# First expert stage of a fused attention and expert kernel: weight loads six units apart, x and Y loaded later, first second-product one unit later, a fourth buffer

## The chip, the cores and the metric

The kernel runs on one core of a Trainium2 chip. The core has five engines with queues of their own, each worked off strictly in order: PE (TensorE, matrix products), DVE (VectorE), ACT (ScalarE), POOL (GpSimd) and SP (SyncE, which here only issues DMAs). The metric is device microseconds of one execution; the time given is the median over several runs.

## The reference

The kernel computes attention with a memory term and, on its output, two expert layers:

```python
x = _attn(q, k, v, M_prev, z_prev, beta)          # 2304 tokens x 512, four batches of 576
h = x @ w_in                                      # 512 -> 2048
x = (h / (1 + exp(-h))) @ w_out                   # 2048 -> 512: the first expert layer
h = x @ w2_in                                     # 512 -> 1024
sm = softmax(h); s = h * sm
out = (layer_norm(s) * g_ln) @ w2_out             # 1024 -> 512: the second expert layer
```

All of it is float32. To run products on PE at full rate, each float32 operand is split into two parts (`xh` and `xl`, `gh` and `glo`, `w[:, :, 0]` and `w[:, :, 1]`), and each product is made of three: high by high, low by high, high by low.

## The kernel before

The first expert layer is cut by the hidden dimension into 16 chunks `f` of 128 columns (`w_in` and `w_out` of a chunk lie in one tile `w`). A **unit** is one chunk for 288 tokens (half a batch): `h_unit` makes the first product (12 matmuls into `psh`), ACT applies the activation in place and casts to `gh`, and DVE subtracts to `glo`; `m1_y` makes the second product (12 matmuls into four banks `psy0` to `psy3`: 8 with `gh`, then 4 with `glo`). Over the chunks of a **part** the four banks accumulate; after the part's last chunk they are added to `Y[b]` in SBUF (four DVE instructions `y<-y,psy`; four ACT copies in the very first part; the last two parts use another form for the activation). There is one set of four banks, so the first second-product of the next half-part can start only when these four adds are done. The list `work` holds 92 units, numbered 0 to 91 below: units 0 to 11 are chunks 0 to 5 of batch 3 (the other batches' chunks 0 to 5 were done during the attention, their sums wait in DRAM as `Yd`), units 12 to 51 are chunks 6 to 10 of all batches (half-parts of five units), 52 to 75 chunks 11 to 13 (three units), 76 to 91 chunks 14 and 15 (two units).

A chunk's weights come by `load_w` in two halves: a DMA into `wraw` (pool `wr`, two buffers), an ACT instruction and three DVE instructions that unpack the raw words into `wf` (`TENSOR_SCALAR`, two `SCALAR_TENSOR_TENSOR`), an ACT cast to the high part, a POOL subtraction for the low part; chunks 20 to 23 (second layer's `w_out`) have one more DVE instruction per half, a product with `gl`. The chunks 6 to 15 and the eight of the second layer (16 to 23) go through eleven slots (`w1p`, `w0p`), each of which can be refilled when its old chunk is used up (`free`). `x` of batches 0 and 1 and `Y` of batches 2, 0 and 1 come back from DRAM in this stage. `split_x` casts 288 tokens of x on ACT (`xh`) and subtracts on POOL (`xl`).

The program writes all operations into a list with a due number `order.prio` each; a planner (`Order.plan`) places them: at each step the engine whose next operation can start first, and on it the operation that can start first by a cost table, ties by the lower due number. What results is one fixed order per engine. The lines that the change touches:

```python
        while st["w"] < len(coming) and n + 1 >= free[st["w"]]:
            next_w()
            if n % 3:
                break
```

Of the kernel before, what the change touches and what calls it, by code (L numbers as in the profile page):

```python
# [17 lines left out]
PSUM = bass.MemoryType.PSUM  # L18
DRAM = bass.MemoryType.DRAM
SBUF = bass.MemoryType.SB  # L20
# [18 lines left out]
WARM = (100000, 1, 4000)  # L39
T_S, T_T, T_O = 20, 10.5, 21  # L40
T_A, T_B, T_P, T_G, T_Y, T_C = 8, 4, 2, 1, 2.5, 1
P0 = 6
W1 = 5

# [4 lines left out]
class Sym:  # L49


    def __init__(self, buf, ap, path=()):
        self.buf, self.ap, self.path = buf, ap, path
# [80 lines left out]
class Order:  # L134
# [7 lines left out]
    def __init__(self, scratch):  # L142
        self.scratch, self.made, self.rings, self.ops, self.prio, self.least = scratch, {}, {}, [], 0, 0
        self.walls = []
        self.chain = None

    def stand_in(self, shape, dtype):
        key = (shape, str(dtype))
# [18 lines left out]
    def take(self, eng, real, method, args, kw):  # L167
        outs = [a for i, a in enumerate(args) if isinstance(a, Sym) and (i == 0 or (method == "tensor_tensor_reduce" and i == 7))]
        outs += [a for k, a in kw.items() if k in ("out", "accum_out") and isinstance(a, Sym)]
        every = [a for a in list(args) + list(kw.values()) if isinstance(a, Sym)]  # L170
        ins = [a for a in every if not any(a is o for o in outs)]
        n = len(self.ops)
        deps, raw, bufs = set(), set(), []
        for a in every:
            assert not a.buf.closed, (method, a.buf.name)
            if a.buf not in bufs:
                bufs.append(a.buf)
        for a in ins:
            c = a.cells()
            raw.update(a.buf.writer[c].tolist())  # L180
            a.buf.readers.append((n, c))
        deps.update(raw)
        for a in outs:
            c = a.cells()
            deps.update(a.buf.writer[c].tolist())
            kept = []
            for r, rc in a.buf.readers:
                if r == n:
                    kept.append((r, rc))
                    continue  # L190
                hit = np.isin(rc, c)
                if hit.any():
                    deps.add(r)
                if not hit.all():
                    kept.append((r, rc[~hit]))
            a.buf.readers = kept
            a.buf.writer[c] = n
        deps -= {-1, n}
        if self.chain is not None:

            deps.update(self.chain)
            self.chain = [n]
        reads = deps.intersection(raw)
        for b in bufs:
            b.ops.append(n)
        took, after = self.length(eng, method, args, kw, outs, ins)
        self.ops.append((eng, real, method, args, kw, deps, bufs, took, after, self.prio, self.least, reads))
# [156 lines left out]
def body(ctx, tc, qk, qk2, qt, vp, mz, beta, w1, w2i, w2o, gln, out):  # L364
# [8 lines left out]
    def f32(ap):  # L373
# [17 lines left out]
    order = Order(bacc.Bacc("TRN2", target_bir_lowering=False, num_devices=1))  # L391
    pe, dve, act, pool, sp = (order.engine(n, e) for n, e in (
        ("pe", nc.tensor), ("dve", nc.vector), ("act", nc.scalar), ("pool", nc.gpsimd), ("sp", nc.sync)))
# [5 lines left out]
    def pools(stack, **kinds):  # L399
        return [Pool(order, bufs, space, name=name, **({"side": side} if side else {}))  # L400
                for name, (bufs, space, side) in kinds.items()]
# [6 lines left out]
    xes, att = ExitStack(), ExitStack()  # L408
    kept = pools(ctx, w0p=(P0, SBUF, None), dx=(1, DRAM, None), gates=(1, SBUF, None), xsp=(1, SBUF, None))
    w0p, dx, gates, xsp = kept  # L410
# [104 lines left out]
    st = {}  # L515
    heads, raws, v_t, mem_t, s_t, unit, X, Xd, Yd = {}, {}, {}, {}, {}, {}, {}, {}, {}
# [343 lines left out]
    for b, c0, c1, z0, z1 in FILL:  # L860
        fs = range(PART[b])
        w = [(fill_split, b, c0, c1)] + [(fill_h, f) for f in fs] + [(fill_y, b, c0, c1, fs, c) for c in range(4)]
        fill += [(z0 + (z1 - z0) * n / len(w), *x) for n, x in enumerate(w)]
    ws = sorted((T_W[n] + T_W[2] * i, n, i) for i in range(P0) for n in range(2))
    calls = []
# [8 lines left out]
    for n, (z, d, u, q0, q1) in enumerate(turns):  # L874
        q = (q0, q1)
        due = dict(DUE, **T_2) if q0 else DUE if q1 == S else dict(DUE, **T_1)
        due = {k: x + (T_0 if q1 < S else 0) for k, x in due.items()}
# [11 lines left out]
        while ws and ws[0][0] < z + d:  # L889
            least = WLEAST[0] + WLEAST[1] / 2 * (2 * P0 - len(ws))  # L890
            call(z, ws[0][0] + DUE["w"], load_w, ws[0][2], w0p, p1, (ws[0][1],), least=least)
# [44 lines left out]
    mo, wes = ExitStack(), ExitStack()  # L936
    lasting = pools(ctx, yp=(1, SBUF, None), w1p=(W1, SBUF, None))
    yp, w1p = lasting
    xq, = pools(xes, xq=(1, SBUF, "right"))
    second = pools(mo, wr=(2, SBUF, None), m1=(2, SBUF, None), m3=(3, SBUF, None), m0=(1, SBUF, None), ps_h=(4, PSUM, None), ps_y=(1, PSUM, None))  # L940
    wr, m1, m3, m0, ps_h, ps_y = second

    def open_second():
# [8 lines left out]
    due = 9 * NU + 12  # L952
    order.prio = due
    Y = [yp.tile([128, NP, S], F32, tag=f"y{b}", name="y") for b in range(B)]
    for b in range(2):
        X[b] = xq.tile([128, NP, S], F32, tag=f"x{b}", name="x")
        sp.dma_start(X[b], Xd[b])

    n1 = P0 + W1
    coming = list(range(P0, NF + 8))  # L960
    before = [-1] * W1 + list(range(P0)) + coming[:len(coming) - n1]
    parts = [(b, PART[b], P0) for b in (3, 0, 1, 2) if PART[b] < P0]
    parts += [(b, f, min(f + 3, NF)) for f in (P0, n1) + tuple(range(n1 + 3, NF, 3)) if f < NF for b in (2, 3, 0, 1)]
    parts = [(b, f0, n1 if f0 == P0 else f1) for b, f0, f1 in parts]
    work = [(p, i, f) for p, (b, f0, f1) in enumerate(parts) for i in range(2) for f in range(f0, f1)]
    free = [1 + max(n for n, w in enumerate(work) if w[2] == c) if 0 <= c < NF else 0 if c < 0 else len(work)
            for c in before]
    st = {}

    def next_w():  # L970
# [98 lines left out]

    for _ in range(W1):  # L1070
        next_w()
    for b in (2, 0, 1):
        sp.dma_start(Y[b], Yd[b])
    blocks = list(range(9, NT // 128)) + list(range(9))
    eb = None
    for n, (p, i, f) in enumerate(work):
        due += 1
        ahead = [T_A, T_B].index(len(work) - n) if len(work) - n in (T_A, T_B) else None
        if ahead is not None:
            if eb is None:  # L1080

                eb = xr.tile([128, NP * S], F32, tag="x", name="eb")
                tb = [xr.tile([128, NP * S], F32R, tag="x", name="tb")]
            y = at(due - 5, m2_split, 128 * blocks[ahead])
            hs = at(due, m2_h, *y)
            es.append(at(due + 1, m2_norm, hs, ahead))
        order.prio = due
        if f == parts[p][1]:
            st["xs"] = split_x(turn(), parts[p][0], HS * i, HS * i + HS) if n else ahead_xs
        st["g"] = h_unit(f, st["xs"], ps_h, m3, "", p >= len(parts) - T_P)  # L1090
        order.prio = due + T_Y
        m1_y(p, i, f)
        order.prio = due
        while st["w"] < len(coming) and n + 1 >= free[st["w"]]:
            next_w()
            if n % 3:
                break


    tb.append(xq.tile([128, NP * S], F32R, tag="x0", name="tb"))  # L1100
# [70 lines left out]
```

## Time and profile before

| | us |
|---|---|
| runs before | 918.62, 918.67, 920.16 |
| median | 918.67 |
| profiled execution: span from first to last instruction | 916.1 |
| time around the span (median less span) | 2.57 |

The profiled execution's own time is not listed apart from its span; the span and the 2.57 us around it are taken as its time, which is then the median. In the profile a line number L360 stands for every operation, since the planner's loop issues them all; names such as `psy<-gh,w` (out<-in) tell them apart.

### The profile page before, as it was taken

The numbers are of one execution on the slowest core, as the hardware profiler recorded it, in microseconds if no ns is written. First come the engines' busy times: TensorE is split into PE (matmuls) and PEld (weight loads), VectorE is DVE, ScalarE is ACT, GpSimd is POOL, SyncE is SP. The second block draws the span as 40 slices with busy tenths as digits, with TensorE's granted clock in tenths as the row PEclk, the third lists the DMA queues.
The fourth block names the chain that finished last, engine by engine and source line by source line (L and its number), as shares of the span: only waits on it lengthen the run. The fifth ranks groups of instructions, "written<-read, shape, count | busy, mean of one in ns | idle before, by whom it ended". The sixth has DMA issues, their size and how long they took to land.

```text
span 916.1 us, 15738 instructions
## 1 busy us (share of the span) xinstructions
PE 879.8 (96%) x5762; PEld 802.4 (88%) x5762; DVE 596.7 (65%) x1396; ACT 495.5 (54%) x1201; POOL 402.1 (44%) x334
## 2 busy tenths in 40 slices
PE   8989999999999999999989999999899999999998
PEld 6666889998999999998989999999899888888886
DVE  4777779878777757258785227932656666666663
ACT  5767689878788767455653325434443333332222
POOL 4555588877767754334542216423542111111110
PEclk9999999999999999999999999999999999999999
DMA  7525343433322310364342002300000000000000
GB/s 226 163 86 172 89 160 110 123 135 110 109 89 86 106 36 7 146 254 138 116 136 96 1 1 92 115 24 1 1 1 1 13 24 24 24 23 24 24 24 35
DMA packets 26653, 71.97 MB, mean 79 GB/s; under 512 B 3152, under 2 KB 10064, under 8 KB 25680
## 3 DMA queue, kind: packets, MB, share of 16 engines
q1 hardware_dynamic: 26576, 70.97, 23.6%
q8 instruction: 45, 0.74, 0.3%
q14 instruction: 32, 0.26, 0.1%
HBM read 60.34 MB, written 10.62 MB: 77 GB/s over the span
## 4 chain that ended last, share of the span: by engine, by line
PE 69%; DVE 18%; ACT 6%; issue 4%; DMA 2%; POOL 1%; ACTq 0%; DVEq 0%; SPq 0%; POOLq 0%
PE psh L360 25%; PE pso L360 11%; PE psy L360 10%; DVE wf L360 9%; PE pst L360 5%; PE pss L360 5%; PE psav L360 5%; PE psfy L360 5%; DVE a L360 2%; DVE phe L360 2%; DVE aTl L360 1%; ACT wf L360 1%; PE psr L360 1%; DMA wraw<-in_w 1%; ACT a L360 1%
## 5 line engine op out<-in xcount | busy, mean ns | idle before, releaser
L360 PE MATMUL psh<-xh,w 128*128 128x288 f32 (+2 forms) x1024 | 205.4, 300 | 0.3 <-ACT w L360 0.2
L360 PEld LDWEIGHTS psh<-xh,w 128*128 128x128 f32 x1024 | 161.4, 189 | 3.1 <-ACT aTh L360 0.8
L360 POOL TENSOR_TENSOR xl<-x,xh 128x1152 fp32r<-128x1152 f32 (+3 forms) x35 | 88.5, 2532 | 120.5 <-ACT xh L360 100.7
L360 PE MATMUL psh<-xl,w 128*128 128x288 f32 (+2 forms) x512 | 137.1, 298 | 0.0
L360 PE MATMUL psy<-gh,w 128*128 128x288 f32 x736 | 120.4, 300 | 12.1 <-DVE y L360 10.0
L360 DVE TENSOR_TENSOR glo<-psh,gh 128x288 fp32r<-128x288 f32 (+2 forms) x128 | 57.5, 452 | 110.3 <-ACT gh L360 110.2
L360 PEld LDWEIGHTS psy<-gh,w 128*128 128x128 f32 x736 | 106.4, 192 | 14.5 <-ACT w L360 5.7
L360 POOL TENSOR_TENSOR w<-wf,w 128x512 fp32r<-128x512 f32 x48 | 65.5, 1368 | 94.1 <-ACT w L360 94.1
L360 PE MATMUL pso<-w,tb 128*128 128x512 f32 x432 | 104.0, 397 | 0.0
L360 ACT ACTIVATE a<-a,nm 128x128 f32<-128x128 f32 (+4 forms) x144 | 84.4, 588 | 23.0 <-DVE nm L360 21.9
L360 PEld LDWEIGHTS pso<-w,tb 128*128 128x128 f32 x432 | 79.9, 188 | 17.1
L360 DVE SCALAR_TENSOR_TENSOR wf<-wraw,wf 128x512 uint32<-128x512 uint32 x96 | 92.5, 964 | 3.2
L360 PEld LDWEIGHTS psh<-xl,w 128*128 128x128 f32 x512 | 91.5, 190 | 0.1
L360 PE MATMUL psh<-w,yh 128*128 128x512 f32 x288 | 90.1, 394 | 0.0
L360 DVE CUSTOM_DVE_ANT_0 a<-pss,tri 128x128 f32<-128x128 f32 (+4 forms) x144 | 67.6, 476 | 21.3 <-PE pss L360 17.3
L360 PE MATMUL pst<-ident,a 128*128 128x128 f32 (+1 forms) x400 | 70.2, 281 | 5.0 <-ACT rb L360 2.1
L360 ACT ACTIVATE psh<-psh 128x288 f32<-128x288 f32 x84 | 33.1, 395 | 76.1 <-PE psh L360 75.9
L360 PE MATMUL psy<-glo,w 128*128 128x288 f32 x368 | 69.5, 299 | 2.3 <-DVE glo L360 2.3
L360 DVE TENSOR_TENSOR aTl<-pst,aTh 128x128 fp32r<-128x128 f32 (+3 forms) x120 | 56.2, 483 | 18.7 <-ACT aTh L360 18.2
L360 PE MATMUL psfy<-gh,w 128*128 128x288 f32 (+2 forms) x288 | 63.6, 303 | 1.8 <-ACT w L360 1.7
L360 PEld LDWEIGHTS psh<-w,yh 128*128 128x128 f32 x288 | 53.9, 188 | 12.0
L360 PEld LDWEIGHTS pst<-ident,a 128*128 128x128 f32 (+1 forms) x400 | 46.9, 140 | 13.9 <-ACT a L360 5.5
(129 smaller groups left out, 1905.9 us busy)
## 6 DMA issues: line engine op xcount, KB each, us to landing
wraw<-in_w SPq DMA_DIRECT2D x32, 512.0 KB, 3.7
rawqk<-in_qk SPq DMA_DIRECT2D x24, 608.0 KB, 3.8
rawv<-in_vp SPq DMA_DIRECT2D x16, 320.0 KB, 3.1
out<-ob SPq DMA_DIRECT2D x18, 256.0 KB, 2.0
wraw<-in_w2i SPq DMA_DIRECT2D x8, 512.0 KB, 3.6
wraw<-in_w2o SPq DMA_DIRECT2D x8, 512.0 KB, 3.6
rawq<-in_qt SPq DMA_DIRECT2D x12, 288.0 KB, 2.8
y<-yd SPq DMA_DIRECT2D x3, 1152.0 KB, 14.7
```

What stands on the lines that cost most here:

```text
L360: getattr(target, method)(*[real(a) for a in args], **{k: real(v) for k, v in kw.items()})
```

## The change

The weight loads get a start of their own: after the first five chunks each load starts at unit `max(free - 1, previous + 6, 12)`, where before it was any unit from `free - 1` on, nearly one a unit. X of batches 0 and 1 and Y of batches 2, 0 and 1 were loaded together ahead of unit 0; now each is loaded at a unit of its own (`loads`). While these loads are recorded, `order.gate` makes the planner place the DMA no earlier than the unit's first operation; this is a rule of the planner alone, no wait on the chip. The second product of a half-part's first unit gets a due number one higher. The pool `m3` (tiles `gh` and `glo`) has four buffers in place of three.

```diff
--- before.py
+++ after.py
@@ -39,6 +39,7 @@
 WARM = (100000, 1, 4000)
 T_S, T_T, T_O = 20, 10.5, 21
 T_A, T_B, T_P, T_G, T_Y, T_C = 8, 4, 2, 1, 2.5, 1
+W_FROM, W_EVERY = 12, 6
 P0 = 6
 W1 = 5
 
@@ -143,6 +144,7 @@
         self.scratch, self.made, self.rings, self.ops, self.prio, self.least = scratch, {}, {}, [], 0, 0
         self.walls = []
         self.chain = None
+        self.gate = None
 
     def stand_in(self, shape, dtype):
         key = (shape, str(dtype))
@@ -200,6 +202,9 @@
 
             deps.update(self.chain)
             self.chain = [n]
+        if self.gate is not None and eng == "sp":
+
+            deps.add(self.gate)
         reads = deps.intersection(raw)
         for b in bufs:
             b.ops.append(n)
@@ -937,7 +942,7 @@
     lasting = pools(ctx, yp=(1, SBUF, None), w1p=(W1, SBUF, None))
     yp, w1p = lasting
     xq, = pools(xes, xq=(1, SBUF, "right"))
-    second = pools(mo, wr=(2, SBUF, None), m1=(2, SBUF, None), m3=(3, SBUF, None), m0=(1, SBUF, None), ps_h=(4, PSUM, None), ps_y=(1, PSUM, None))
+    second = pools(mo, wr=(2, SBUF, None), m1=(2, SBUF, None), m3=(4, SBUF, None), m0=(1, SBUF, None), ps_h=(4, PSUM, None), ps_y=(1, PSUM, None))
     wr, m1, m3, m0, ps_h, ps_y = second
 
     def open_second():
@@ -952,9 +957,12 @@
     due = 9 * NU + 12
     order.prio = due
     Y = [yp.tile([128, NP, S], F32, tag=f"y{b}", name="y") for b in range(B)]
-    for b in range(2):
+    def load_x(b):
         X[b] = xq.tile([128, NP, S], F32, tag=f"x{b}", name="x")
         sp.dma_start(X[b], Xd[b])
+
+    def load_y(b):
+        sp.dma_start(Y[b], Yd[b])
 
     n1 = P0 + W1
     coming = list(range(P0, NF + 8))
@@ -965,6 +973,9 @@
     work = [(p, i, f) for p, (b, f0, f1) in enumerate(parts) for i in range(2) for f in range(f0, f1)]
     free = [1 + max(n for n, w in enumerate(work) if w[2] == c) if 0 <= c < NF else 0 if c < 0 else len(work)
             for c in before]
+    starts = []
+    for i, n in enumerate(free):
+        starts.append(0 if i < W1 else max(n - 1, starts[-1] + W_EVERY, W_FROM))
     st = {}
 
     def next_w():
@@ -1069,8 +1080,7 @@
 
     for _ in range(W1):
         next_w()
-    for b in (2, 0, 1):
-        sp.dma_start(Y[b], Yd[b])
+    loads = {6: (load_y, 2), 9: (load_x, 0), 14: (load_y, 0), 19: (load_x, 1), 24: (load_y, 1)}
     blocks = list(range(9, NT // 128)) + list(range(9))
     eb = None
     for n, (p, i, f) in enumerate(work):
@@ -1085,16 +1095,19 @@
             hs = at(due, m2_h, *y)
             es.append(at(due + 1, m2_norm, hs, ahead))
         order.prio = due
+        gate = len(order.ops)
         if f == parts[p][1]:
             st["xs"] = split_x(turn(), parts[p][0], HS * i, HS * i + HS) if n else ahead_xs
         st["g"] = h_unit(f, st["xs"], ps_h, m3, "", p >= len(parts) - T_P)
-        order.prio = due + T_Y
+        order.prio = due + T_Y + (f == parts[p][1])
         m1_y(p, i, f)
         order.prio = due
-        while st["w"] < len(coming) and n + 1 >= free[st["w"]]:
+        order.gate = gate
+        if n in loads:
+            loads[n][0](loads[n][1])
+        while st["w"] < len(coming) and n >= starts[st["w"]]:
             next_w()
-            if n % 3:
-                break
+        order.gate = None
 
 
     tb.append(xq.tile([128, NP * S], F32R, tag="x0", name="tb"))
```

The number and kinds of instructions on each engine are the same; their order differs from the first expert stage on. Three places:

DVE at the end of the half-part of units 22 to 26 (`glo` is one unit's subtraction, `wf` rows are a weight half, the four `y` rows add the half-part's sums). Before:

```order
L360 TENSOR_TENSOR glo<-psh,gh 128x288
L360 TENSOR_SCALAR wf<-wf 128x512
L360 SCALAR_TENSOR_TENSOR wf<-wraw,wf 128x512 x2
L360 TENSOR_TENSOR glo<-psh,gh 128x288
L360 TENSOR_TENSOR y<-y,psy_6505 128x288
L360 TENSOR_TENSOR y<-y,psy_6511 128x288
L360 TENSOR_TENSOR y<-y,psy_6536 128x288
L360 TENSOR_TENSOR y<-y,psy_6543 128x288
L360 TENSOR_SCALAR wf<-wf 128x512
L360 SCALAR_TENSOR_TENSOR wf<-wraw,wf 128x512 x2
```

With the change:

```order
L365 TENSOR_TENSOR glo<-psh,gh 128x288 x3
L365 TENSOR_TENSOR y<-y,psy_6504 128x288
L365 TENSOR_TENSOR y<-y,psy_6508 128x288
L365 TENSOR_TENSOR y<-y,psy_6511 128x288
L365 TENSOR_TENSOR y<-y,psy_6514 128x288
L365 TENSOR_TENSOR glo<-psh,gh 128x288 x2
L365 TENSOR_SCALAR wf<-wf 128x512
L365 SCALAR_TENSOR_TENSOR wf<-wraw,wf 128x512 x2
L365 TENSOR_SCALAR wf<-wf 128x512
L365 SCALAR_TENSOR_TENSOR wf<-wraw,wf 128x512 x2
```

Before, a weight half stands ahead of the last `glo` and the four adds; with the change three `glo` and the four adds stand with no weight row ahead of them, and a whole chunk follows two units later. On PE, one first product (12 matmuls) stood between a half-part's last second product and the next half-part's first one; with the change two stand there, at nearly every such place.

SP, the DMA queue, from the last store of the attention's sums on (`wraw` is a weight half, `x` and `y` a batch's tile of 1152 KB). Before:

```order
L360 DMA yd<-yo 128x288 x8
L360 DMA x<-xd 128x2304 x2
L360 DMA wraw<-in_w 128x1024 x2
L360 DMA y<-yd 128x2304 x3
L360 DMA wraw<-in_w 128x1024 x18
L360 DMA wraw<-in_w2i 128x1024 x8
```

With the change, from the first weight halves on:

```order
L365 DMA wraw<-in_w 128x1024 x2
L365 DMA y<-yd 128x2304
L365 DMA wraw<-in_w 128x1024 x5
L365 DMA x<-xd 128x2304
L365 DMA wraw<-in_w 128x1024 x5
L365 DMA y<-yd 128x2304
L365 DMA wraw<-in_w 128x1024 x2
L365 DMA x<-xd 128x2304
L365 DMA y<-yd 128x2304
L365 DMA wraw<-in_w 128x1024 x6
L365 DMA wraw<-in_w2i 128x1024 x8
```

Before, both x and all three Y were issued around the first two weight halves; now they stand between later halves, and SP reaches each only after the half in front of it, which waits until its buffer has been unpacked.

ACT around units 84 and 85, where the second expert layer begins (`eb` is its exponential, `g` the other form of the activation, `ACT_TABLE_LOAD` the switch between function tables, `wf` and `w` of chunk 23). Before:

```order
L360 CAST xh<-x 128x1152
L360 ACT_TABLE_LOAD
L360 ACTIVATE eb,m<-psh_8687,m 128x512
L360 ACTIVATE g<-psh 128x288
L360 ACTIVATE eb,m<-psh_8707,m 128x512
L360 CAST gh<-psh 128x288
L360 CAST yh<-y 128x4x128
L360 ACTIVATE g<-psh 128x288
L360 CAST gh<-psh 128x288
```

With the change:

```order
L365 ACTIVATE wf<-wraw 128x512 x2
L365 CAST w<-wf 128x512
L365 CAST xh<-x 128x1152
L365 ACTIVATE g<-psh 128x288
L365 CAST w<-wf 128x512
L365 CAST gh<-psh 128x288
L365 CAST yh<-y 128x4x128
L365 ACT_TABLE_LOAD
L365 ACTIVATE eb,m<-psh_8674,m 128x512
L365 ACTIVATE eb,m<-psh_8692,m 128x512
L365 ACTIVATE g<-psh 128x288
L365 CAST gh<-psh 128x288
```

Chunk 23 now stands here, the table load has moved behind the cast of unit 84 and a cast of y, and both exponentials stand ahead of unit 85's `g` and `gh`. On PE, unit 85's second product for bank 0, which needs that `gh`, now stands ahead of unit 86's first product; before, it stood behind unit 87's.

## Rows read from the trace of the kernel before

**Rows 1.** Page of the profiled execution: its span and the busy time of each engine

```profile
span 916.1 us, 15738 instructions
...
PE 879.8 (96%) x5762; PEld 802.4 (88%) x5762; DVE 596.7 (65%) x1396; ACT 495.5 (54%) x1201; POOL 402.1 (44%) x334
```

**Rows 2.** Busy us by stretch (start:end, us), granted TensorE clock, DMA share, GB/s

```profile
379.79:666.94 287.15, 272.66 (x1994) 269.62 (x1993) 164.44 (x272) 134.04 (x272) 109.48 (x59) 0.98 0.26 88
420.00:500.00 80.00, 71.25 (x500) 69.39 (x500) 62.67 (x94) 41.71 (x85) 34.53 (x21) 0.96 0.38 125
```

**Rows 3.** The same stretch, instructions on psy alone, then on psh alone

```profile
379.79:666.94 287.15, 149.11 (x984) 138.44 (x984) 28.37 (x73) 2.70 (x8) 0.98 0.26 88
...
379.79:666.94 287.15, 149.81 (x1008) 140.13 (x1009) 37.44 (x83) 65.69 (x167) 0.98 0.26 88
```

**Rows 4.** Chain that ended last, 505:556: start us, us, what

```profile
511.79 1.60 PE psh L360 x12
...
550.00 1.61 PE psh L360 x12
```

**Rows 5.** Waits of PE, 378:720: us in total, times, longest us

```profile
PE psy L360 <- DVE y L360: 10.0, 5, 3.5
PE psy L360 <- DVE glo L360: 2.3, 1, 2.3
PE psy L360 <- ACT y L360: 1.7, 1, 1.7
```

**Rows 6.** Columns of Rows 2, around two waits of PE

```profile
424.00:428.00 4.00, 2.27 (x15) 1.93 (x15) 3.59 (x6) 2.62 (x7) 1.75 (x1) 1.00 0.37 131
...
462.00:464.00 2.00, 2.00 (x11) 1.99 (x11) 1.95 (x2) 0.57 (x2) 1.44 (x1) 0.60 0.64 240
464.00:466.00 2.00, 2.00 (x11) 1.97 (x10) 1.80 (x5) 1.21 (x2) 0.56 (x1) 0.54 0.20 20
```

**Rows 7.** DVE in time: start us, us, instruction, idle before it

```profile
480.70 1.42 DVE L360 SCALAR_TENSOR_TENSOR wf<-wraw,wf 128x512 uint32<-128x512 uint32 x2
482.40 1.54 DVE L360 TENSOR_TENSOR y<-y,psy 128x288 f32<-128x288 f32 x4
```

**Rows 8.** DVE and POOL in time where both run, two places

```profile
470.82 3.79 DVE L360 SCALAR_TENSOR_TENSOR wf<-wraw,wf 128x512 uint32<-128x512 uint32 x2
...
471.14 2.92 POOL L360 TENSOR_TENSOR xl<-x,xh 128x1152 fp32r<-128x1152 f32 x1 [0.64 <-ACT xh L360]
...
566.90 1.53 DVE L360 TENSOR_TENSOR y<-y,psy 128x288 f32<-128x288 f32 x4
...
566.02 3.12 POOL L360 TENSOR_TENSOR xl<-x,xh 128x1152 fp32r<-128x1152 f32 x1
```

**Rows 9.** DVE instructions by form, 380:720: busy us, mean ns, idle before

```profile
L360 DVE SCALAR_TENSOR_TENSOR wf<-wraw,wf 128x512 uint32<-128x512 uint32 x72 | 71.8, 997 | 2.4
L360 DVE TENSOR_TENSOR y<-y,psy 128x288 f32<-128x288 f32 x80 | 31.4, 446 | 7.0 <-PE psy L360 6.9
```

**Rows 10.** Page, DMA issues: KB each, us to landing

```profile
wraw<-in_w SPq DMA_DIRECT2D x32, 512.0 KB, 3.7
y<-yd SPq DMA_DIRECT2D x3, 1152.0 KB, 14.7
```

**Rows 11.** PE and ACT in time, 666:678

```profile
666.94 0.62 PE L360 MATMUL psh<-w,yh 128*128 128x512 f32 x2
...
672.51 0.43 PE L360 MATMUL psh<-xh,w 128*128 128x288 f32 x2
...
673.71 1.28 ACT L360 ACT_TABLE_LOAD   x1
675.00 0.69 ACT L360 ACTIVATE eb<-psh,m 128x512 f32<-128x512 f32 x1
676.63 0.41 ACT L360 CAST gh<-psh 128x288 fp32r<-128x288 f32 x1
677.42 0.62 ACT L360 CAST yh<-y 128x512 fp32r<-128x512 f32 x1 [0.38 <-PE psh L360]
```

## The prediction

> **What bounds the kernel now.** The page first: PE is busy for 879.8 us of a span of 916.1 [rows 1], so time can only be won where PE waits or runs slowly. The change touches one stage, from unit 0 (379.79 us) to the start of the second layer's first product (666.94), so I cut that out [rows 2]: 287.15 us long, PE busy for 272.66, mean granted clock 0.98. In 420:500 PE is busy for 71.25 of 80 and DVE for 62.67. What should the stage take? It holds 984 + 1008 = 1992 matmuls of 288 columns [rows 3]. Where nothing disturbs, 24 groups of 12 lie between 511.79 and 550.00 us [rows 4]: 38.21 / 288 = 0.1327 us each. So 1992 x 0.1327 = 264.3 us, and **22.9 us are lost**.
>
> The waits say to whom [rows 5]. Of 14 us that PE waits, 10.0 in five waits are for DVE's adds `y`, 2.3 for a `glo`, 1.7 for ACT's copies of y. The adds themselves are short: 1.54 us for four [rows 7]. They come late because DVE works its queue in order, and weight rows stand ahead: at 480.70 a half's pair takes 1.42 us, and the adds start only at 482.40. A clean half costs DVE about 1.9 us with its first instruction; but the pair's instruction takes 997 ns on average [rows 9] where half of 1.42 is 710.
>
> The clock is the second loss: after the wait at 461 us PE runs for four microseconds at 0.60 and 0.54 of full clock [rows 6], that is mostly at 1.2 and no longer at 2.4 GHz, which costs 2 x 0.40 + 2 x 0.46 = 1.7 us. Three of the waits are followed by such a dip of 1.7 us; others are not, as at 424:428, where PE is busy for only 2.27 of 4 us and the clock stays at 1.00. So 14 + 3 x 1.7 = 19 of the 22.9 us are named; the rest is the pipe that drains and fills around each wait.
>
> **The change part by part.**
>
> *Loads six units apart.* A unit is 24 matmuls, 3.18 us; six are 19.1 us. In them DVE now has one chunk (two halves, 2 x 1.9 us, 5 to 6 with what POOL holds it up), six `glo` and one or two groups of adds: some 11 of 19. Before, in 420:500, it had 62.67 of 80. At the end of the half-parts no weight row stands ahead of the adds from unit 17 to unit 75, but for a few places where the chunk began two units earlier and is done.
>
> *First second-product one unit later.* PE now has two first products, 3.18 us, between the last product of a half-part and the first that needs the banks free; before it had 1.59. The adds need 1.54 plus about 0.4 for the two semaphores, so 1.59 was only just enough with DVE free, and 3.18 leaves 1.2 us. Together these two remove the five waits for `y`, the one for `glo` and the dips that follow: all 22.9 us but what comes back below. Nothing is added: the same instructions run on every engine.
>
> *Fourth buffer.* With two first products in a row, four units' `gh` and `glo` are alive; with three buffers unit n would wait for the second product of n - 3. It costs no time by itself; it is what lets the step above work.
>
> *x and Y later.* Two x no longer lie ahead of the first weight half, so chunk 6 can be unpacked during units 2 and 3 and not 4 to 6. The first y is asked for at unit 0 to 6 and added after unit 16; the others are issued by about unit 15 and first used at units 32 to 46. Hidden, with 50 us and more to spare.
>
> *New waits at the start (units 5 to 12).* The first six chunks still come as fast as two `wraw` buffers allow: a half lands 3.7 us after its issue [rows 10], and ACT then holds everything behind it until a half has landed or has been unpacked. I followed ACT, DVE and POOL instruction by instruction with durations from the trace and find two tight places. At unit 5 ACT's cast of chunk 7's second half waits for DVE, and `gh` of unit 5 is queued behind it. If POOL's `xl` of the next half-part starts first, DVE's pair is stretched as at 470.82, where it takes 3.79 us and not 1.42 beside a POOL instruction of 2.92 [rows 8]; then PE waits 0.9 us. At unit 12 the four ACT copies of y stand behind two weight instructions of ACT: 1.2 us. Bounds: nothing, and 3.1 if both are a microsecond worse. I take 1.7, with the first at half its price, as either of the two can start first.
>
> The Trainium skill, SBUF — State Buffer, section "Who interferes with whom", has a rule for that first place: a VectorE instruction with two SBUF inputs and a GpSimd instruction that reads SBUF exclude each other, the one that starts second waiting for the whole of the first. The trace agrees with it: the pair at 470.82 ends when `xl` has ended and one more instruction has run, while four adds, which have one input in PSUM, keep 1.53 us beside an `xl` [rows 8]. By the rule the place costs 0.9 in full or nothing, by order of start; the sum above takes the middle.
>
> *New wait at units 84 to 87.* Chunk 23 now comes here. Count from the start of the second layer's product, t = 0. That product ends at 672.51 - 666.94 = 5.57 [rows 11]; units 84 and 85 and second products 82 and 83 are 48 matmuls, so PE is at 11.9 where it needs bank 0, and at 12.3 where it needs `gh` of unit 85. DVE ends its adds at 1.4, then chunk 23: four instructions of the pair and four shorter ones, 4.6 us, with one wait for POOL about 5.7, then two reductions; at 8.4 it has made unit 84 ready for ACT's cast. ACT: `gh` of unit 84 until 8.9, a cast of y 0.6, the table load 1.28, two exponentials with their reads of the sum 1.8, unit 85's `g` 0.4 [rows 11]: 12.9. DVE's half microsecond and ACT's cast follow, 13.95, and PE goes on at 14.2: **a wait of 2.2 us**. The last bank's add comes 0.3 us late. Before, units 84 to 87 lost 0.6 us here, so the change costs 2.0 net. At units 88 to 91, without a table load, the third bank's add is 0.6 us late. Bounds: nothing, if POOL does not hold DVE and the reductions start at 6; 5, if POOL holds it for both halves and a clock dip follows.
>
> The Trainium skill, ScalarE: Activation LUTs, section "What ACT_TABLE_LOAD costs", gives 2.66 us for a switch, load and drain. The trace does not bear the drain out: the load at 673.71 takes 1.28 and the exponential starts at 675.00 [rows 11]. By the page's figure this wait would be 1.4 us longer and the sum 902.4.
>
> *Clock.* A wait of 2.2 us was followed by a dip in about half of the cases before, so 0.5 x 1.7 = 0.9.
>
> **Sum.** The profiled execution is taken as 918.67, the median: its span of 916.1 and 2.57 around it. 918.67 - 22.9 + 1.7 + 2.0 + 0.6 + 0.9 = **901.0 us**.
>
> **The rivals.**
>
> *Clean (12 in 100).* No new wait at all: POOL never starts first, and the end of the stage keeps its slack. 918.67 - 22.9 = 895.8 us. Against it: the exponentials now stand ahead of unit 85's cast, and that order does not depend on luck.
>
> *More comes back (20 in 100).* The two tight places at the start and both at the end cost their upper bounds, 3.1 + 5 + 0.7, with a clock dip after one wait at the start, 1.7, and one more place in the short half-parts (units 52 to 83, where a chunk's eight to ten DVE instructions and the adds lie within 9.6 us) loses 2: 895.8 + 12.5 = 908 us. For it: 997 against 710 ns shows how much POOL can hold DVE [rows 9].
>
> *No change (3 in 100).* The change does not do what it says: the waits for `y` come from DVE's slowness beside POOL and not from the order. Then DVE would stay late with a third of the work, which the undisturbed stretch 511.79 to 550.00 speaks against, where the same `xl` runs every five units. 918 us.
>
> *Slower (4 in 100).* x or Y late. In SP's queue x of batch 0 stands behind five weight halves, each of which waits until a buffer is unpacked; x of batch 1 and the last Y stand behind twelve. ACT's cast of that x for unit 32 would then hold every activation behind it, and PE with them. It decides from the point where x lands 23 us after its need. Against it: five halves at some 4 us each put the issue near 405 us, the need is at 379.8 + 32 x 3.18 = 482 us, and the slowest group of loads, the three Y asked for together, took 14.7 us in the median [rows 10]. To turn the sign a load would have to take over 80 us longer. 925 us.
>
> **Chances and range.** 61 in 100 for the forecast, whose own range is 898 to 905; the rest as above. A measurement of this kernel can tell 0.2%, 1.8 us. Faster by more: 61 + 12 + 20 = 93; within: 3; slower: 4. The range reaches over the clean case with half a microsecond to spare and to the middle of the case where more comes back: 895 to 909.
>
> **What would show it.** In the changed profile the waits of PE for `y<-y,psy` between units 17 and 83 should be gone, and unit n should follow unit n - 1 by 3.18 us; the granted clock should read 1.00 from unit 17 on. The stage should be 265 to 268 us long up to the second layer's first product, the steps behind it 2 to 3 us longer than before, with one PE wait of about 2 us for `gh` of unit 85 or bank 0. DVE's weight pairs should still be longer than 1.42 us beside POOL. I am wrong if waits for adds stay in the half-parts of five units (then order was not the cause), if ACT waits for `wraw` with PE behind it all through the first twenty units, or if a wait for x appears at unit 32 or 42.

## The result, and the profile after

The changed kernel takes 899.66 us (median of four runs, 899.22 to 900.41), the kernel before, beside it, 919.41: ratio 0.9784, 95% interval 0.9770 to 0.9798. The forecast was 901.0, with a range of 895 to 909. The profiled execution has 899.22 us around a span of 897.4; before it was a span of 916.1 [rows 1].

The first two rows of the page; DVE's busy time falls by 10.3 us though it runs the same 1396 instructions:

```profile
span 897.4 us, 15717 instructions
...
PE 873.2 (97%) x5762; PEld 797.8 (89%) x5762; DVE 586.4 (65%) x1396; ACT 493.9 (55%) x1201; POOL 402.2 (45%) x334
```

Busy us by stretch, in the columns of [rows 2]: the stage up to the second layer's first product (now at 647.07), units 84 to 87 with that product, units 88 to 91 with the next, and 420:500:

```profile
379.79:647.07 267.28, 265.94 (x1992) 264.67 (x1990) 149.28 (x265) 130.60 (x271) 107.78 (x57) 1.00 0.28 94
647.07:667.15 20.08, 18.56 (x122) 17.32 (x121) 16.66 (x38) 9.43 (x17) 9.60 (x7) 1.00 0.00 1
667.15:685.51 18.36, 18.36 (x122) 17.29 (x121) 12.49 (x31) 7.07 (x16) 7.39 (x5) 1.00 0.01 1
...
420.00:500.00 80.00, 79.73 (x598) 79.26 (x597) 41.48 (x71) 37.22 (x80) 27.88 (x16) 1.00 0.32 110
```

In 420:500 PE was busy for 71.25 of 80 us and is now for 79.73; DVE fell from 62.67 to 41.48; the clock stands at 1.00. PE's first product of unit 0 starts at 379.41 here, 0.38 earlier than before. So the account is: 0.38 us are won ahead of the stage; the stage goes from 287.15 to 647.07 - 379.41 = 267.66, that is 19.5 won; units 84 to 87 go from 18.91 to 20.08, 1.2 lost; the next stretch is nearly as before. Together that is 18.7, the difference of the spans.

What PE still waits for in 378:720 (us in total, times, longest), beside [rows 5], and the four waits with their place (start, length, instruction, idle time before it):

```profile
PE psy L365 <- ACT gh L365: 1.9, 2, 1.5
PE psy L365 <- DVE y L365: 0.6, 1, 0.6
PE psy L365 <- ACT y L365: 0.2, 1, 0.2
```

```profile
400.69 1.32 PE L365 MATMUL psy<-gh,w 128*128 128x288 f32 x8 [0.37 <-ACT gh L365]
425.49 1.43 PE L365 MATMUL psy<-gh,w 128*128 128x288 f32 x8 [0.25 <-ACT y L365]
637.21 1.04 PE L365 MATMUL psy<-gh,w 128*128 128x288 f32 x5 [0.58 <-DVE y L365]
660.69 0.51 PE L365 MATMUL psy<-gh,w 128*128 128x288 f32 x2 [1.52 <-ACT gh L365]
```

14 us of waits have become 2.7. The first, second and fourth stand where the prediction put them: unit 5, unit 12, units 84 and 85. The third, at the second product of unit 78 (the expectations below call it unit 80, by its place in time), was not foreseen. Its chain shows what is still at work; POOL, DVE and ACT in time:

```profile
631.82 3.15 POOL L365 TENSOR_TENSOR xl<-x,xh 128x1152 fp32r<-128x1152 f32 x1
```

```profile
632.71 2.55 DVE L365 TENSOR_SCALAR wf<-wf,gl 128x512 f32<-128x512 f32 x1
636.24 0.46 DVE L365 TENSOR_TENSOR glo<-psh,gh 128x288 fp32r<-128x288 f32 x1 [0.99 <-ACT gh L365]
636.62 1.54 DVE L365 TENSOR_TENSOR y<-y,psy 128x288 f32<-128x288 f32 x4
```

```profile
635.29 0.62 ACT L365 CAST w<-wf 128x512 fp32r<-128x512 f32 x1 [3.34 <-DVE wf L365]
635.81 0.40 ACT L365 CAST gh<-psh 128x288 fp32r<-128x288 f32 x1
```

A scaling of a weight half that takes 0.48 us elsewhere takes 2.55 and ends just after POOL's `xl`. ACT's copy of that half waits 3.34 us for it, `gh` is queued behind the copy, DVE's `glo` behind `gh`, the adds behind `glo`, and PE behind the adds. The weight rows are no longer crowded, yet DVE is held as before; so the experiments had to part the order from the hold.

### The profile page after: what moved, and what is told of

Same layout as the page of the kernel before. It is cut to its first block, busy times and chain, and to the rows that moved or that the text cites. A ratio compares the mean times of both kernels' runs of the same rounds, so it can differ in the third digit from the quotient of the medians.

```text
span 897.4 us, 15717 instructions
## 1 busy us (share of the span) xinstructions
PE 873.2 (97%) x5762; PEld 797.8 (89%) x5762; DVE 586.4 (65%) x1396; ACT 493.9 (55%) x1201; POOL 402.2 (45%) x334
## 4 chain that ended last, share of the span: by engine, by line
PE 76%; DVE 13%; ACT 5%; issue 3%; DMA 2%; POOL 0%; SPq 0%; ACTq 0%; DVEq 0%
PE psh L365 28%; PE psy L365 14%; PE pso L365 11%; PE pst L365 5%; PE pss L365 5%; PE psav L365 5%; PE psfy L365 5%; DVE wf L365 4%; DMA wraw<-in_w 2%; DVE a L365 2%; DVE phe L365 2%; DVE aTl L365 1%; PE psr L365 1%; ACT a L365 1%; PE psm L365 1%
## 5 line engine op out<-in xcount | busy, mean ns | idle before, releaser
L365 PE MATMUL psh<-xh,w 128*128 128x288 f32 (+2 forms) x1024 | 202.3, 298 | 0.0
L365 PE MATMUL psy<-gh,w 128*128 128x288 f32 x736 | 114.8, 296 | 2.8 <-ACT gh L365 1.9
L365 PEld LDWEIGHTS psy<-gh,w 128*128 128x128 f32 x736 | 103.4, 188 | 4.3 <-ACT gh L365 3.1
L365 DVE SCALAR_TENSOR_TENSOR wf<-wraw,wf 128x512 uint32<-128x512 uint32 x96 | 82.8, 863 | 3.1
L365 DVE TENSOR_TENSOR aTl<-pst,aTh 128x128 fp32r<-128x128 f32 (+3 forms) x120 | 56.2, 483 | 18.7 <-ACT aTh L365 18.3
L365 PE MATMUL psy<-glo,w 128*128 128x288 f32 x368 | 65.2, 295 | 0.0
L365 ACT CAST w<-wf 128x512 fp32r<-128x512 f32 x48 | 29.7, 620 | 57.3 <-DVE wf L365 56.5
```

Source lines behind the costliest of these rows:

```text
L365: getattr(target, method)(*[real(a) for a in args], **{k: real(v) for k, v in kw.items()})
```

## Experiments

Two theories. **Order**: weight rows ahead of the adds in DVE's queue make PE wait, and spacing them is the cure. **Hold**: DVE's weight rows are long because POOL holds DVE (an instruction of DVE that meets one of POOL's is done only after POOL's has ended); without that the old order costs nothing. Beside them stands the question which of the four parts of the change carries the gain. The before-kernel's median moves by 0.2% between the sets of runs, so ratios to it are compared; 0.001 is 0.92 us.

| kernel | us | ratio to before, 95% interval |
|---|---|---|
| the change | 899.66 | 0.9784, 0.9770 to 0.9798 |
| e1_old_pace | 924.98 | 1.0051, 1.0035 to 1.0067 |
| e2_no_delay | 911.77 | 0.9904, 0.9889 to 0.9920 |
| e3_three_bufs | 899.00 | 0.9773, 0.9754 to 0.9793 |
| e4_xy_first | 903.39 | 0.9815, 0.9798 to 0.9832 |
| e5_spacing_only | 908.41 | 0.9865, 0.9852 to 0.9878 |
| e6_delay_only | 922.66 | 1.0022, 1.0012 to 1.0033 |
| e7_before_no_low | 896.14 | 0.9734, 0.9721 to 0.9747 |
| e8_after_no_low | 899.09 | 0.9772, 0.9754 to 0.9789 |
| e10_before_short_pool | 896.67 | 0.9735, 0.9721 to 0.9748 |
| e11_before_short_w | 902.34 | 0.9795, 0.9782 to 0.9809 |
| e9_last_at_80 | 902.07 | 0.9798, 0.9783 to 0.9813 |
| e12_last_at_74_80 | 902.00 | 0.9788, 0.9768 to 0.9809 |

### One part undone at a time

**e1_old_pace**, against the changed kernel:

```diff
-        while st["w"] < len(coming) and n >= starts[st["w"]]:
-            next_w()
         order.gate = None
+        while st["w"] < len(coming) and n + 1 >= free[st["w"]]:
+            next_w()
+            if n % 3:
+                break
```

> The changed kernel, with the weight loads of the kernel before (a chunk as soon as its buffer is free, nearly one per unit); the later second product, the fourth buffer and the late x and Y stay. Theory 'order' (weight rows ahead of the adds in DVE's queue make PE wait): DVE's queue again has the four weight halves of chunks 12 and 13 between the adds of unit 18 and others at 23, 28 and 53 to 61, so most of the gain goes: 909 to 917 us, with several waits of PE for y<-y,psy back in 420:500 and 550:590. Rival 'cover' (the later second product alone carries the gain, as it gives the adds 3.18 and not 1.59 us): 900 to 904 us and no such wait over 1 us.

Measured: 924.98 us, 4.7 us **above** the kernel before by the ratio, and beyond what either theory gave. PE's waits:

```profile
PE psy L365 <- DVE y L365: 12.8, 7, 3.7
PE psy L365 <- DVE glo L365: 5.3, 2, 2.9
```

The chain that ended last (start, us, what) now runs for some 70 us over the weights themselves; a piece of it:

```profile
439.00 0.70 DVE wf L365
439.73 1.65 DVE wf L365
...
441.43 4.62 DMA wraw<-in_w
```

A half's buffer comes free only when DVE has read it; then the next half needs 4.62 us to land; then ACT and DVE again. Of the two equal instructions in a row one takes 0.70, the other 1.65: that is the hold. So the spacing is needed, and the three other parts together, without it, do harm.

**e2_no_delay**:

```diff
-        order.prio = due + T_Y + (f == parts[p][1])
+        order.prio = due + T_Y
```

> The changed kernel without the one-unit delay of each part's first second product; spacing, fourth buffer, late x and Y stay. Theory 'order': with the weight rows spaced, the adds follow their last product at once, and 1.59 us are just enough for 1.54 us of adds, as they were in the undisturbed units of the kernel before; only the three or four places where a weight half stands between two adds (units 37, 55, 61) and the steps at unit 84 lose: 901 to 905 us. Rival 'cover': every half-part loses 0.3 to 0.5 us or more, 20 of them 6 to 10 us: 906 to 911 us.

Measured: 0.9904, 11 us above the change; with the result's kernel before, 919.41, that is 910.6 us, at the upper end of the rival's range and far above the first theory's. The waits (start, length, instruction, idle before it) are of three kinds, and one of each is shown:

```profile
426.99 0.79 PE L365 MATMUL psy<-glo,w 128*128 128x288 f32 x4 [2.66 <-DVE glo L365]
...
610.39 1.53 PE L365 MATMUL psy<-gh,w 128*128 128x288 f32 x8 [0.97 <-DVE y L365]
...
674.41 0.53 PE L365 MATMUL psy<-gh,w 128*128 128x288 f32 x2 [1.39 <-DVE y L365]
```

A `glo` behind weight rows at the start, with the clock at 0.80 for eight microseconds behind it (1.6 us); five places at 512, 570, 590, 610 and 631 us where a weight half stands among the adds, 3.45 us in all; and 2.7 at units 84 to 87. The time is the rival's, the places are not: the other half-parts lose nothing, as the first theory had it, but it put the price at less than half. DVE and POOL ahead of the first:

```profile
419.87 2.51 DVE L365 TENSOR_SCALAR wf<-wf 128x512 uint32<-128x512 uint32 x1 [1.16 <-ACT wf L365]
422.41 1.42 DVE L365 SCALAR_TENSOR_TENSOR wf<-wraw,wf 128x512 uint32<-128x512 uint32 x2
423.75 0.42 DVE L365 TENSOR_SCALAR wf<-wf 128x512 uint32<-128x512 uint32 x1
424.20 2.36 DVE L365 SCALAR_TENSOR_TENSOR wf<-wraw,wf 128x512 uint32<-128x512 uint32 x2
426.49 0.81 DVE L365 TENSOR_TENSOR glo<-psh,gh 128x288 fp32r<-128x288 f32 x2
```

```profile
419.40 2.69 POOL L365 TENSOR_TENSOR xl<-x,xh 128x1152 fp32r<-128x1152 f32 x1
424.56 1.45 POOL L365 TENSOR_TENSOR w<-wf,w 128x512 fp32r<-128x512 f32 x1 [2.47 <-ACT w L365]
```

The first instruction of a half takes 2.51 us beside `xl` and 0.42 without POOL; the pair 2.36 beside `w` and 1.42 without. Again it is a held row that makes the `glo` late.

**e3_three_bufs**: `m3=(4, SBUF, None)` is made `m3=(3, SBUF, None)`.

> The changed kernel with three and not four buffers for gh and glo. PE's order is the same; ACT's gh of unit n waits for the second product of unit n-3. If the fourth buffer is what lets the later second product work (as the prediction had it), each of some 20 half-parts loses up to 0.3 us: 903 to 907 us. Rival: ACT has a second product's 1.6 us to spare there and the buffer does nothing for the time: 899 to 901 us, PE's waits as in the changed kernel.

Measured: 0.9773, the same as the change; PE's waits agree within 0.3 us. The rival holds: the fourth buffer does nothing for the time.

**e4_xy_first**:

```diff
+    for b in range(2):
+        load_x(b)
...
+    for b in (2, 0, 1):
+        load_y(b)
-    loads = {6: (load_y, 2), 9: (load_x, 0), 14: (load_y, 0), 19: (load_x, 1), 24: (load_y, 1)}
+    loads = {}
```

> The changed kernel with x and Y loaded as in the kernel before: both x ahead of the first weight half, the three Y behind the first five chunks. If late x and Y do nothing but let chunk 6 come earlier: the first chunks are unpacked some 3 us later, during units 4 to 12, and the start loses 0 to 3 us: 899.5 to 903 us, the stage from unit 17 on at the same pace of 3.18 us a unit. Rival: the loads ahead of the weights are a main part of the gain: 905 us or more, with PE waiting for gh behind weight rows of ACT in units 5 to 16.

Measured: 0.9815, 2.9 us above the change: the upper end of the first theory. The difference lies at the start, mostly in two waits of PE (the change has 0.25 there); from 450 us on the waits are those of the change:

```profile
426.86 0.40 PE L365 MATMUL psh<-xh,w 128*128 128x288 f32 x1 [1.71 <-ACT w L365]
...
446.47 1.26 PE L365 MATMUL psy<-gh,w 128*128 128x288 f32 x6 [0.88 <-DVE y L365]
```

### One part alone

**e5_spacing_only**, against the kernel before: the diff's `W_FROM, W_EVERY`, `starts`, `gate` and the loop, and nothing else.

> The kernel before with the spaced weight loads alone; second products not delayed, three buffers, x and Y loaded first as before. Theory 'order, and cover where rows still meet': DVE's queue is that of before up to the adds of unit 18 and that of the changed kernel without the delay from unit 30 on, so it loses what the run without the delay lost (12 us above the changed kernel) and up to 4 us at the start, and keeps one wait of before at units 17 to 23: 910 to 916 us. Rival: each of the parts gains by itself and the gains add; then the spacing alone, taken from the run with the old pace (25 us above the changed kernel), brings all: 900 us or less.

Measured: 0.9865, 12.4 us below the kernel before and 7.5 above the change, a little better than expected. Of the waits of before, those at 425 and 445 us are still there (1.66 and 1.42 us) and the later ones are gone; the five small places of the run without the delay are there, and 1.6 us at units 84 to 87.

Beside e2 this run shows something that the single steps hide. e2 has the same spacing and no delay, but late x and Y and the fourth buffer, and it is 3.6 us slower (0.9904 against 0.9865): its wait of 2.66 us at 426.99, and the low clock behind it, do not occur here. So late x and Y, which gain 2.9 us where the second product is delayed (e4), seem to cost time where it is not; the fourth buffer was not parted from them in this pair.

**e6_delay_only**, against the kernel before:

```diff
-m3=(3, SBUF, None)
+m3=(4, SBUF, None)
...
-        order.prio = due + T_Y
+        order.prio = due + T_Y + (f == parts[p][1])
```

> The kernel before with each part's first second product one unit later and with the fourth buffer alone; the old pace of the weights, x and Y loaded first. Theory: the weight rows stay in front of the adds in units 17 to 30 and 53 to 62, and 1.6 us more of cover is less than one weight half beside POOL takes on DVE (some 3 us), so little is won: 912 to 919 us, waits of PE for y of 1 us and more still there. Rival 'cover': 901 to 906 us.

Measured: 1.0022, slower than before by 2 us. Nothing was won; PE waits 9.7 us for the adds in seven waits, where it was 10.0 in five [rows 5]. So the delay is worth nothing with the old pace and 11 us with the spacing: the parts do not add up, each is worth what the other lets it be.

### Order or hold

**e7_before_no_low** and **e8_after_no_low**: in the stage, POOL's two subtractions are left out.

```diff
-            pool.tensor_tensor(w[:, n, 1], f32(f), f32(w[:, n, 0]), ALU.subtract)
+            if low:
+                pool.tensor_tensor(w[:, n, 1], f32(f), f32(w[:, n, 0]), ALU.subtract)
...
-        xl = pl.tile([128, NP, c1 - c0], F32R, tag="xl", name="xl")
+        xl = pl.tile([128, NP, c1 - c0], F32R, tag="xl", name="xl") if low else xh
```

> The kernel before, with POOL's work left out in the stage: the low parts xl and w are not computed, the products read the high parts in their place (same count and shape of matmuls, other numbers). Tests the rival 'no change' of the prediction, that DVE is late because POOL holds it and not because of the order. If POOL alone is the cause: DVE's pair takes 1.4 us everywhere, all waits for y go, 896 to 900 us. If the order alone is: 912 to 919 us. Mine: both; weight rows still stand among the adds, but each half holds them 1.9 and not 3 to 4 us, so half of the 20 us goes: 904 to 911 us.

> The changed kernel with the same left out (the low parts xl and w of the stage, the high parts read in their place). With rows spaced and DVE not held, the small waits at units 5 and 12 and at 80 go, and the wait at unit 85 is shorter by what POOL holds DVE there: 897 to 899 us. If POOL plays no part in what is left: 899.5 us as with POOL.

Measured: 896.14 and 899.09 us. The kernel **before**, with POOL idle in the stage, is faster than the change: PE has one wait of 0.26 us in 378:720, and the clock is 1.00. My middle value of 904 to 911 was wrong; without POOL's work the whole loss is gone. And the change with POOL idle is no faster than with it (0.9772 against 0.9784): it is 3.5 us behind the old order, of which 2.6 are two waits of its own order, 1.78 for ACT's copies of y at unit 12 and 0.8 at units 84 and 85.

**e10_before_short_pool** and **e11_before_short_w**: in e7 the planner, with POOL empty, had put a few adds in other places. Here it plans with the old lengths and the old dependencies; every engine's order is that of the kernel before, only POOL's instructions are narrower.

```diff
+            order.scale = 512 // low
-            pool.tensor_tensor(w[:, n, 1], f32(f), f32(w[:, n, 0]), ALU.subtract)
+            pool.tensor_tensor(w[:, n, 1, :low], f32(f[:, :low]), f32(w[:, n, 0, :low]), ALU.subtract)
+            order.scale = 1
...
-            return 145 + 2.11 * n, 0
+            return 145 + 2.11 * n * self.scale, 0
```

> The kernel before with every engine's instructions in exactly its order, but with POOL's xl and w in the stage an eighth as wide (36 of 288 and 64 of 512 columns); the products read the high parts where these were read, so the numbers differ and the count and shape of matmuls do not. In the run without POOL's low parts the planner had also put the adds of units 17 to 24 in other places; here it has not. If the order by itself makes PE wait, even with DVE unheld: 905 us or more, PE waits for y at units 17 to 24. If it is POOL's hold on DVE that makes the rows long: 896 to 899 us, DVE's weight rows near 0.42 and 0.69 us, hardly a wait.

> The same with only w (the chunks' low parts, 1.3 us each, 36 in the stage) an eighth as wide, xl as in the kernel before (2.9 us each, 17 in the stage). By the time that POOL reads, w is 47 us and xl 50; but each w runs while DVE converts the next half, so if hold goes by meeting, w does most of it: 900 to 906 us. If the long xl does most: 910 to 917 us.

Measured: 896.67 and 902.34 us. The same order that loses 22.9 us costs two waits of a quarter of a microsecond once POOL's instructions are short (e10):

```profile
PE psy L365 <- DVE mv L365: 0.3, 1, 0.3
PE psy L365 <- DVE y L365: 0.2, 1, 0.2
```

DVE's weight rows in 378:720 (count, minimum, median and maximum in ns), before, then with all of POOL's work narrow:

```profile
L360 DVE SCALAR_TENSOR_TENSOR wf<-wraw,wf x72: 681/693/3166, 393.1 to 649.1; 128x512 uint32<-128x512 uint32 x72
L360 DVE TENSOR_SCALAR wf<-wf x36: 416/563/2217, 392.6 to 648.0; 128x512 uint32<-128x512 uint32 x36
```

```profile
L365 DVE SCALAR_TENSOR_TENSOR wf<-wraw,wf x72: 672/693/747, 394.5 to 628.6; 128x512 uint32<-128x512 uint32 x72
L365 DVE TENSOR_SCALAR wf<-wf x36: 414/427/741, 394.0 to 627.5; 128x512 uint32<-128x512 uint32 x36
```

The busy time of all 116 weight rows on DVE in 378:720 (second number; one row each of the kernel before, e5 with the spacing alone, the change, e11 and e10):

```profile
378.00:720.00 342.00, 104.07 (x116) 0.99 0.22 74
```

```profile
378.00:720.00 342.00, 100.48 (x116) 1.00 0.21 75
```

```profile
378.00:720.00 342.00, 92.36 (x116) 1.00 0.22 76
```

```profile
378.00:720.00 342.00, 82.63 (x116) 1.00 0.22 76
```

```profile
378.00:720.00 342.00, 68.77 (x116) 1.00 0.22 76
```

Unheld, the rows take 68.8 us; before they took 104.1, so POOL held them for 35.3. The change brings the hold to 23.6 and puts what remains where little waits for it. The spacing alone leaves 31.7 us of hold and still wins 12.4 us: most of what it does is to give the held rows room, not to make them shorter. Narrow `w` alone takes away 104.07 - 82.63 = 21.4 of the 35.3 us of hold and brings the ratio to 0.9795 where all brings it to 0.9735, that is 18.9 of 24.4 us: the short `w` of 1.3 us does more harm here than the long `xl`. What a narrow `xl` alone would bring was not run. What the runs leave open: a narrow POOL instruction also ends earlier, so a part of the gain may be that buffers (`wf`, `xl`) come free sooner. Before, in 378:720, ACT sat idle for POOL's `w` for 1.4 us in two waits, and DVE not at all, so that part should be small.

### A version that might beat the change

**e9_last_at_80** and **e12_last_at_74_80**, against the changed kernel (the second with 74 in place of 78):

```diff
+    starts[-2:] = [78, 80]
     st = {}
```

> The changed kernel with the last chunk's load started at unit 80 and not 84, so that its eight DVE instructions and ACT's copies lie between the adds of units 79 and 81, ahead of the exponentials' table load. If that chunk's place makes the wait of 1.5 us at unit 85: that wait goes or shrinks to the 0.3 us of the kernel before, and up to 0.6 us comes back at units 81 to 83: 897.5 to 899.2 us. If the wait comes from the table load and the exponentials alone: 899.5 to 900.5 us, the wait still there.

> The same with the chunk before the last started at unit 74 and not 78 too: its rows stand between g of 74 and the adds of 76, not around the adds of 76 to 79, which should remove the wait of 0.6 us at unit 80: 896.8 to 899 us. If that wait only moves to the adds of 76 or 79: as the run with the last chunk at 80 alone.

Measured: 0.9798 and 0.9788, neither better than the change. e9 missed both of its ranges; e12 came out like e9, its second alternative, though the wait moved to another place than was said. The wait at units 84 and 85 goes, as the theory said, to 0.33 and 0.34; but another appears, in e9 for adds behind the last chunk's rows and in e12 for a `glo` (one row of each):

```profile
646.56 1.53 PE L365 MATMUL psy<-gh,w 128*128 128x288 f32 x8 [1.66 <-DVE y L365]
```

```profile
629.65 0.80 PE L365 MATMUL psy<-glo,w 128*128 128x288 f32 x4 [1.95 <-DVE glo L365]
```

At both places that were tried the wait was moved and not removed; whether a better one exists was not shown.

## Why the prediction was right, and where it was not

**Right: what was lost and could be had back.** 22.9 us were counted as lost in the stage. The runs with POOL idle or narrow give 896.1 and 896.7 us, against the 895.8 of the clean case; by their ratios they lie 24.4 us below the kernel before, 1.5 more than was counted. The count was made from PE's own pace, so it did not depend on what makes the adds late, and the forecast could come out right with the cause in part wrong.

**Right in effect, wrong in cause.** The prediction said that the adds "come late because DVE works its queue in order, and weight rows stand ahead". They stand ahead, but e10 has the same order and hardly a wait: the order costs time only where the rows are held. The step that failed is the dismissal of DVE's slowness beside POOL, as the rival called no change: "the undisturbed stretch 511.79 to 550.00 speaks against, where the same `xl` runs every five units". In that stretch DVE had no weight row at all, so there was nothing to hold, and POOL had no `w`, whose narrowing alone brings back 18.9 of 24.4 us. The rival's cause was right and its time wrong: spaced rows have room to be late (e5), and in the changed kernel they are also held less (23.6 us, not 35.3). The trace of before held the answer: 72 instructions at 997 ns on average against 710 [rows 9] are 20.7 us, and [rows 8] shows how they come about.

**Rightly seen: the rule of the Trainium skill.** SBUF — State Buffer, section "Who interferes with whom", on which the term at unit 5 was weighed, states the rule behind the hold: of a VectorE and a GpSimd instruction that contend, the one that starts second waits for all of the other. It names `tensor_scalar` too, in its two-port modes; the runs agree (0.42 us alone, 2.51 beside `xl`). The prediction applied the rule to one place and 0.9 us, where it ruled the stage.

**The delay and the spacing.** "Together these two remove the five waits": they did, and neither does it alone. The delay alone is worth -2 us, the spacing alone 12.4.

**Fourth buffer.** "It is what lets the step above work": wrong, three do as well (e3).

**x and Y later.** No price had been given beyond an earlier chunk 6; by e4 it is 2.9 us, at the start, with the delay in place.

**The terms that came back.** Start: 1.7 forecast, 0.37 + 0.25 = 0.6 of waits measured; at unit 12 PE waited 0.25 us for the copies of y and not 1.2. The wait of 0.58 at unit 78 was not in the sum, though a place lost in the short half-parts was part of the rival in which more comes back. Over the 264.3 the stage loses 267.66 - 264.3 = 3.4, of which 1.2 are these three waits. Most of the other 2 us lies around the same waits, where the products before and behind a wait are late as well: from start to start PE loses 0.6 us at unit 5, 0.4 at unit 6 (406 us), 0.5 at unit 12, 0.3 at 470 us and 0.9 at unit 78. By this count the start, units 5 to 12, costs 1.5 and not 0.6. Units 84 to 87: 2.0 forecast, 1.2 measured. The mechanism was the one described; PE went on 660.69 - 647.07 = 13.6 us after the product's start and not 14.2. ACT, then DVE's add of bank 0, which ends with `gh` of unit 85 (start, length, instruction):

```profile
656.59 1.28 ACT L365 ACT_TABLE_LOAD   x1
657.89 0.69 ACT L365 ACTIVATE eb<-psh,m 128x512 f32<-128x512 f32 x1
...
659.23 0.41 ACT L365 ACTIVATE g<-psh 128x288 f32<-128x288 f32 x1
660.16 0.40 ACT L365 CAST gh<-psh 128x288 fp32r<-128x288 f32 x1 [0.53 <-DVE psh L365]
```

```profile
660.11 0.43 DVE L365 TENSOR_TENSOR y<-y,psy 128x288 f32<-128x288 f32 x1
```

The table load takes 1.28 us again and the exponential follows 0.02 later. The Trainium skill, ScalarE: Activation LUTs, section "What ACT_TABLE_LOAD costs", would have had 1.4 us more here; the trace does not show them. Units 88 to 91: 0.6 forecast, nothing measured (18.36 us, 18.40 before). Clock: 0.9 forecast, no dip. The sum: 3.4 + 1.2 measured against 1.7 + 2.0 + 0.6 + 0.9 forecast; it came out near because the stage lost more than forecast and the steps behind it less, which is luck.

**What would show it.** Unit follows unit by 3.18 us, the clock is 1.00, the stage is 267.7 long (265 to 268 was said), the wait at unit 85 is 1.5 (about 2). The steps behind grew by 1.2 and not by 2 to 3, and one wait for adds stayed, 0.58 us at unit 78. DVE's rows are still stretched beside POOL. The sign "waits for adds stay in the half-parts of five units (then order was not the cause)" did not appear, but it could not have parted the two causes: spacing the rows takes held rows away from the adds as well.

## What to carry to other kernels

When instructions of one engine take longer on average than alone, find who runs beside the long ones before reading the queue's order as the cause; then test it with the order kept and the suspect made short. If the neighbour can't be moved, spacing the work and giving the consumer more cover can hide most of the hold; here the spacing alone brought 12.4 us and the cover alone nothing, and the whole gain needed both. And a stretch with no victim in it is no evidence that the suspect is harmless.

## What the runs showed of the hardware

POOL's hold is not in proportion to the size of what is held: in the changed kernel, at unit 84, DVE combines two maxima, 128x1. Beside POOL's `xl` that takes 1.35 us and ends at 656.60, `xl` at 656.58; an addition of the same shape takes 0.16 at 659.37 (DVE, then POOL):

```profile
655.25 1.35 DVE L365 TENSOR_TENSOR m<-m 128x1 f32<-128x1 f32 x1
...
659.37 0.16 DVE L365 TENSOR_TENSOR m<-m 128x1 f32<-128x1 f32 x1 [2.21 <-ACT eb L365]
```

```profile
653.89 2.69 POOL L365 TENSOR_TENSOR xl<-x,xh 128x1152 fp32r<-128x1152 f32 x1 [0.47 <-ACT xh L365]
```

The adds `y<-y,psy`, which read one input from PSUM, were never held: none of the 80 took more than 0.46 us in any trace, though in the kernel before 24 of them ran beside a POOL instruction. Of the clock: two stretches of eight microseconds, in each of which PE is busy for 6.3 us with one long wait of 1.66 (e9) and of 1.95 us (e12); columns as in [rows 2], PE alone:

```profile
644.00:652.00 8.00, 6.34 (x40) 1.00 0.00 0
```

```profile
628.00:636.00 8.00, 6.35 (x36) 0.79 0.32 110
```

In the one the clock stays at 2.4 GHz throughout, in the other it reads 0.79 on average, so it was at 1.2 GHz for a part. Nor does the length of the wait sort them: in the kernel before, a wait of 1.83 us that ended at 461.75 was followed by the lower clock [rows 6], and one of 2.29 us that ended at 651.20 was not. What decides is not shown here.
